# A one-token attention and MLP kernel: where the two sets of sums of the output projection meet

## The chip, the cores and the metric

The kernel runs on one core of a Trainium2 chip. The metric is the device time of one execution in microseconds (us). The profile names the engines PE (TensorE, matrix products; PEld is its weight load), DVE (VectorE), ACT (ScalarE), POOL (GpSimd) and SP (SyncE, which here only issues DMAs). A "q" behind an engine's name, as in SPq or DVEq, is that engine's instruction sequencer.

## The reference

One token `x` of 1024 numbers is normalised; an attention block and an MLP block work on the result, and both are added to `x`. Cut to what matters:

```
def reference(A_x, A_k_cache, A_v_cache, A_wq, A_wo, B_x, B_w1, B_b1, B_w2, B_b2):
    # attention: 32 query heads on 4 kv heads of 128, the last W = 4096 cache places
    #   q = xn @ wq;  p = softmax(q k^T / sqrt(128));  o = p v;  A = o @ wo
    # MLP:  y = layernorm(xn);  h = gelu(y @ w1 + b1);  B = h @ w2 + b2
    x = A_x
    xn = _layernorm(x, axis=-1)
    return x + _A_ref(xn, A_k_cache, A_v_cache, A_wq, A_wo) + _B_ref(xn, B_w1, B_b1, B_w2, B_b2)
```

`wo` is 4096 x 1024 and `w2` 3584 x 1024, both bf16. All that the output is made of ends in products of a vector with these two matrices, plus `x` and `b2`.

## The kernel before

The weights and the used parts of the caches pass through SBUF once, some 40 MB in all. SyncE issues the large loads, in this order: w1, k, wq, then (after w1 has been used) w2 and v, then (after wq has been used) wo. ScalarE issues three small loads at the start (x, b1, b2; L206 to L208). TensorE's products have the activation vector as the stationary operand, one column of it in each of 32-column strips of the array, and the matrix streams through. The functions `put`, `tile` and `full` all make their products in one line, L336: `put` uses a strip of 32 columns, so that four products in four strips can run side by side, and `full` uses all 128.

**The output projection.** wo lies in SBUF as 32 "rows", each with 128 partitions and the 1024 outputs. A row is a term of a sum with 32 terms. The rows are loaded in chunks of 16, 8, 4, 2, 1 and 1 (`WO_CHUNKS`, loaded at L193 by `load_rows`), each with a semaphore of its own, `s_wo[j]`. TensorE takes them in three ways:

- The first 24 rows run in a loop (`steps("wo", ...)`, L562), 8 at a time. SyncE releases them at L560 and L561.
- Rows 24 to 27 (chunk 2) are written out. With `row` each is two products of 512 outputs, into the accumulators `acc[0]` and `acc[1]`. These lie in two strips of partitions in PSUM bank 7 and also hold `x`, `b2` and the MLP's sums. When row 27 is done, `C["most"]` is marked.
- Rows 28 to 31 (chunks 3, 4 and 5) are four products of 256 outputs each, into `quad`, four strips of 32 partitions in the first 256 columns of PSUM bank 0. The first products into it carry the flag `start`, which resets the sums. The condition, `j == HALVES`, holds for both rows of chunk 3, 28 and 29, so that row 29 resets what row 28 has left, and row 28 isn't in the sum. The last mark is `C["fin"]`.

**The end** stands after a branch that is never taken. ScalarE copies `acc[0]` in two halves to the first two strips of 32 partitions of `PART` (an fp32 view of SBUF that lies in the tensor `KV`), and VectorE `acc[1]` to the last two (L587 and L588). Both wait for `C["most"]` only. VectorE then waits for ScalarE's copies, its own and `C["fin"]` (L589 to L591), adds `quad` and `PART` (L592) and writes `ORow` in bf16. SyncE waits for that and stores four partitions of `ORow` with 256 numbers each to the output (L594), and the program ends when the store has landed (L595).

`identf` is a 128 x 128 identity matrix in fp32, made at the start by GpSimd (L238 and L239) and used as weights or operand at L492, L501 and L534. The products at L534 (`turn_over`) write a bank that nothing reads afterwards.

Of the kernel before, what the change touches and what calls it, by code (L numbers as in the profile page):

```python
# [6 lines left out]
ALU = mybir.AluOpType  # L7
ACTF = mybir.ActivationFunctionType
# [14 lines left out]
WO_CHUNKS = [16, 8, 4, 2, 1, 1]  # L23
LOOPED = 2
HALVES = 3
# [26 lines left out]
def bass_parallel_sum__sliding_block_cached__mixer_channel_mlp__decode_kernel(  # L52
# [18 lines left out]
    pe, dve, act, pool, sp = nc.tensor, nc.vector, nc.scalar, nc.gpsimd, nc.sync  # L71

    def sems(name, n):
        return [nc.alloc_semaphore(f"{name}{i}") for i in range(n)]

    s_xrow, s_b1, s_b2, s_w1, s_w2, s_out, s_go, s_row = (
        nc.alloc_semaphore(n) for n in ("s_xrow", "s_b1", "s_b2", "s_w1", "s_w2", "s_out", "s_go", "s_row"))
# [5 lines left out]
    PE = Track(nc, "S_PE")  # L83
    DVE = Track(nc, "S_DVE")
    ACT = Track(nc, "S_ACT")
    POOL = Track(nc, "S_POOL")

    def sb(name, shape, d):
        return nc.alloc_sbuf_tensor(name, shape, d)
# [3 lines left out]
    identf = sb("identf", [128, 128], f32)  # L93
# [20 lines left out]
    ORow = sb("ORow", [128, 256], bf16)  # L114
# [21 lines left out]
    PART = KV[:, 4096:4608].bitcast(f32)  # L136
# [5 lines left out]
    PS = nc.alloc_psum_tensor("PS", [128, 8 * 512], f32)  # L142
# [9 lines left out]
    out_rows = out.rearrange("b s (a n) -> (b s a) n", a=4)  # L152

    C = {}
# [70 lines left out]
    def product(out, a, b, ready):  # L225
# [32 lines left out]
        out=SAME[:, :].rearrange("p (h b) -> p h b", b=4), in0=HD[:, 0:32].unsqueeze(2).to_broadcast([128, HQ, 4]),  # L258
        in1=HD[:, 32:64].unsqueeze(2).to_broadcast([128, HQ, 4]), op=ALU.add))
    parts = identf[:, :].rearrange("p (i q h) -> p i q h", i=NPAIR, q=4)  # L260
    POOL.mark(pool.tensor_tensor(out=HD[:, 64:128].rearrange("p (i q h) -> p i q h", i=NPAIR, q=2),
                                 in0=parts[:, :, 0:2, :], in1=parts[:, :, 2:4, :], op=ALU.add))
    pool.wait_ge(POOL.sem, POOL.cnt)
    HD4 = HD[:, 64:128].rearrange("p (i q h) -> p i q h", i=NPAIR, q=2)
    for i in range(NPAIR):
        C["consts"] = POOL.mark(pool.tensor_tensor(
            out=E4[:, :].rearrange("p (q r) -> p q r", r=129)[:, :, 64 * i:64 * i + 64:4],
            in0=HD4[:, i, 0, :].unsqueeze(1).to_broadcast([128, 4, 16]),
            in1=HD4[:, i, 1, :].unsqueeze(1).to_broadcast([128, 4, 16]), op=ALU.add))
# [65 lines left out]
    def tile(out, lhsT, rhs, size, at, load=True, start=False):  # L335
        return pe.add_instruction(mybir.InstMatmult(  # L336
            name=nc.get_next_instruction_name(), engine=pe.engine,
            ins=[lowered(rhs, False), lowered(lhsT, True)], outs=[pe.lower_ap(out)],
            start_tensor_calc=start, stop_tensor_calc=True, bass_skip_group_check=True, ldweights=load,
            tile_size=size, tile_position=at))  # L340

    def put(out, lhsT, rhs, a, load=True, start=False):
        return tile(out, lhsT, rhs, (128, 32), (0, 32 * a), load, start)

    def full(out, lhsT, rhs, load, start=False):
        return tile(out, lhsT, rhs, (128, 128), (0, 0), load, start)
# [99 lines left out]
    for eng, track, qs in ((dve, DVE, (0, 1)), (act, ACT, (2, 3))):  # L446
        eng.wait_ge(PE.sem, C["rep"])
        eng.wait_ge(POOL.sem, C["lb"])
        for q in qs:
            dst = LB8[32 * q:32 * q + 32, :, 32 * q:32 * q + 16]  # L450
            src = PS[32 * q:32 * q + 32, 6 * 512:6 * 512 + 128].rearrange("p (e h) -> p e h", e=8)
# [3 lines left out]
    def row(vec, lo, hi):  # L455
        put(acc[0], vec, lo, 0)
        return put(acc[1], vec, hi, 1)
# [10 lines left out]
    acc = [PS[32 * a:32 * a + 32, 7 * 512:8 * 512] for a in range(2)]  # L468
# [16 lines left out]
    for a in range(2):  # L485
        for i in range(2):
            src = XBR[0:1, i * D + a * 512:i * D + (a + 1) * 512]
            tile(acc[a], identb[0:1, 0:32], src, (32, 32), (0, 32 * a), i == 0, i == 0)

    for half in range(2):  # L490
# [8 lines left out]
                                       in_=MXH[:, :].unsqueeze(1).to_broadcast([1, 4, HQ]), func=ACTF.Copy))  # L499
# [5 lines left out]
    for n in range(4):  # L505
        C["exp"] = ACT.mark(act.activation(  # L506
            out=Pb[:, n * 512:(n + 1) * 512], in_=PS[:, n * 512:(n + 1) * 512], func=ACTF.Exp,
# [3 lines left out]
            out=PT.rearrange("p (i c h) -> p c i h", i=NPAIR, h=16)[:, 16 * n:16 * n + 16],  # L511
            in_=Pb[:, n * 512:(n + 1) * 512].rearrange("p (c i h) -> p c i h", i=NPAIR, h=16)))
# [27 lines left out]
    for c in range(1, 4):  # L540
        C["d_od"] = DVE.mark(dve.scalar_tensor_tensor(  # L541
            out=OD[:, :], in0=PS[:, 4 * 512 + 128 * c:4 * 512 + 128 * c + 128], scalar=BLK[:, c:c + 1], in1=OD[:, :],
# [6 lines left out]
    for dq in range(4):  # L549
# [7 lines left out]
        out=OT, in0=PS[:, 6 * 512 + 160:6 * 512 + 192], scalar1=REC[:, 0:1], scalar2=None, op0=ALU.mult))  # L557
# [7 lines left out]
    for j in range(LOOPED, len(WO_CHUNKS)):  # L565
        pe.wait_ge(s_wo[j], 16)
        for c in range(c0, c0 + WO_CHUNKS[j]):
            if j < HALVES:
                last = row(VEC[:, FC + PAD + c:FC + PAD + c + 32], WA[:, c * D:c * D + 512], WA[:, c * D + 512:(c + 1) * D])
            else:  # L570
                for a in range(4):
                    last = put(quad[a], VEC[:, FC + PAD + c:FC + PAD + c + 32], WA[:, c * D + a * 256:c * D + (a + 1) * 256], a,
                               start=(j == HALVES))
        c0 += WO_CHUNKS[j]
        if j == HALVES - 1:
            C["most"] = PE.mark(last)
    C["fin"] = PE.mark(last)

    pe.br_lt(zero, 0, on_true="L_main", on_false="L_end").branch_hint(ending)
    nc.switch_bb("L_end")  # L580

    for a in range(4):
        eng, track = ((act, ACT), (dve, DVE))[a // 2]
        eng.wait_ge(PE.sem, C["most"])
        dst = PART[32 * a:32 * a + 32, :]
        src = acc[a // 2][:, 256 * (a % 2):256 * (a % 2) + 256]
        C["part", a // 2] = track.mark(act.activation(out=dst, in_=src, func=ACTF.Copy) if eng is act  # L587
                                      else dve.tensor_copy(dst, src))  # L588
    dve.wait_ge(ACT.sem, C["part", 0])  # L589
    dve.wait_ge(DVE.sem, C["part", 1])  # L590
    dve.wait_ge(PE.sem, C["fin"])  # L591
    C["d_out"] = DVE.mark(dve.tensor_tensor(out=ORow[:, :], in0=PS[:, 0:256], in1=PART[:, :], op=ALU.add))  # L592
    sp.wait_ge(DVE.sem, C["d_out"])
    sp.dma_start(out_rows, ORow[0:128:32, :]).then_inc(s_out, 16)  # L594
    sp.wait_ge(s_out, 16)  # L595

    return nc

# [27 lines left out]
```

## Time and profile before

| what | value |
|---|---|
| median of 3 runs | 99.83 us (99.83 to 100.0) |
| profiled execution | 99.88 us |
| its span, first to last instruction | 98.6 us |
| TensorE busy | 53.6 us (54%) |
| VectorE busy | 32.8 us (33%) |
| ScalarE busy | 10.0 us (10%) |
| SyncE's DMA queue, share of 16 engines' span | 94.9% |
| read from HBM | 39.86 MB, 404 GB/s over the span |

Times in the profile count from the span's start. Busy time is summed for each engine and says nothing of order; the chain of waits goes from the last instruction back to what released it and shows what set the end. A line such as `L336` is a line of the kernel's source. In a row of the timeline the first number is the start, the second the length, and the brackets say how long the engine had been idle and what ended that. The ends of products on TensorE are modelled, not measured.

### The profile page before, as it was taken

The page shows a single profiled execution, that of the slowest core. Times are in us where ns is not written, and L with a number is a line of the kernel's source. Part 1 is how long each engine was busy: PE and PEld are TensorE (multiplying, and loading weights), DVE is VectorE, ACT ScalarE, POOL GpSimd, SP SyncE. Part 2 cuts the span into 40 slices and gives each one's busy share as a digit, 9 for nine tenths or more (in the row PEclk, how much of TensorE's full clock was granted, in tenths as well). Part 3 has the DMA queues.
Part 4 walks back from the last instruction along what each step waited for, and adds up shares of the span by engine and source line. Part 5 has one row for each costly group of instructions (what it writes and reads, how often), then busy time and mean ns, then how long its engine had stood idle before and what let it go on. Part 6 is the DMA issues. An engine that isn't in the chain of part 4 may idle for free.

```text
span 98.6 us, 970 instructions
## 1 busy us (share of the span) xinstructions
PE 53.6 (54%) x377; PEld 18.6 (19%) x297; DVE 32.8 (33%) x45; ACT 10.0 (10%) x24; POOL 10.1 (10%) x34
## 2 busy tenths in 40 slices
PE   0420300059920700760086599976999997485860
PEld 0320000012210000100010212213345544042310
DVE  0237100000799999992002300451900004100031
ACT  0506000000040000000002200005700000000030
POOL 2128996000000000000000000000000000000000
PEclk9999999999995555579556957996559999999998
DMA  9798888999999999999988899959999999999960
GB/s 373 326 422 372 373 372 372 465 425 432 425 525 439 425 425 425 425 425 425 585 372 372 372 419 674 395 213 425 425 425 425 425 425 439 425 445 402 401 227 1
DMA packets 2060, 39.86 MB, mean 404 GB/s; under 512 B 262, under 2 KB 266, under 8 KB 652
## 3 DMA queue, kind: packets, MB, share of 16 engines
q1 hardware_dynamic: 2024, 39.85, 94.9%
q10 hardware_dynamic: 36, 0.01, 0.0%
HBM read 39.86 MB, written 0.00 MB: 404 GB/s over the span
## 4 chain that ended last, share of the span: by engine, by line
DMA 88%; SPq 4%; PE 4%; issue 1%; DVE 0%; DVEq 0%
DMA WW<-in_A_wq_dram 47%; DMA WW<-in_A_wo_dram 41%; PE PS L336 4%; SPq L193 3%; SPq L201 1%; DVE ORow L592 0%; SPq L210 0%; DVEq L591 0%; SPq L372 0%
## 5 line engine op out<-in xcount | busy, mean ns | idle before, releaser
L328 DVE STREAM_TRANSPOSE KV<-KV 128x2048 bf16<-128x2048 bf16 x8 | 18.5, 2310 | 15.1 <-DMA KV<-in_A_k_cache_dram 14.9
L336 PE MATMUL PS<-WW,VEC 128*32 (+2 forms) x128 | 16.7, 421 | 4.1 <-SPq L560 1.7
L336 PE MATMUL PS<-WW,XNTb 128*32 x64 | 7.1, 623 | 12.0 <-SPq L372 12.0
L336 PE MATMUL PS<-WW,YTb 128*32 x56 | 6.3, 580 | 10.1 <-DMA WW<-in_B_w_dram 10.1
L336 PEld LDWEIGHTS PS<-WW,VEC 128*32 (+1 forms) x128 | 6.9, 107 | 14.2 <-issue 8.1
L336 PE MATMUL PS<-KV,LB 128*128 128x512 bf16 x32 | 8.8, 442 | 0.7 <-DVE LB L452 0.7
L480 DVE TENSOR_REDUCE MXP<-PS 128x1 f32<-128x1024 f32 x2 | 2.4, 1224 | 7.7 <-PE PS L336 7.7
L336 PEld LDWEIGHTS PS<-WW,XNTb 128*32 x32 | 1.2, 114 | 18.4 <-issue 18.4
L336 PEld LDWEIGHTS PS<-WW,YTb 128*32 x32 | 1.7, 121 | 14.9 <-issue 14.8
L541 DVE SCALAR_TENSOR_TENSOR OD<-PS,BLK,OD 128x128 f32<-128x128 f32 x3 | 1.1, 351 | 10.0 <-ACT OD L538 9.9
L588 DVE COPY KV<-PS 32x256 f32<-32x256 f32 x2 | 0.8, 420 | 10.3 <-PE PS L336 10.3
L336 PE MATMUL PS<-OUTM,PAR 2*128 2x512 bf16 x4 | 1.9, 615 | 3.5 <-DVE HT L399 3.5
L336 PE MATMUL PS<-KV 128*64 x32 | 3.6, 380 | 0.0
L429 DVE CAST Qs<-PS 128x512 bf16<-128x512 f32 x1 | 0.7, 691 | 8.4 <-PE PS L336 8.4
L510 DVE STREAM_TRANSPOSE KV<-KV 128x512 bf16<-128x512 bf16 x4 | 2.7, 711 | 2.0 <-ACT KV L506 2.0
L336 PEld LDWEIGHTS PS<-KV,LB 128*128 128x128 bf16 x16 | 1.8, 110 | 7.1 <-issue 6.3
L506 ACT ACTIVATE KV<-PS,BIAS 128x512 bf16<-128x512 f32 x4 | 2.7, 686 | 0.0
L336 PE MATMUL PS<-KV,oneb 1*32 1x512 bf16 x7 | 1.0, 611 | 3.0 <-DMA KV<-in_B_b_dram 3.0
L427 ACT ACTIVATE Qs<-PS 128x512 bf16<-128x512 f32 x1 | 0.6, 597 | 20.4 <-PE PS L336 20.4
L375 ACT ACTIVATE Hs<-PS 128x512 bf16<-128x512 f32 x1 | 0.6, 597 | 18.1 <-PE PS L336 18.1
L217 POOL TENSOR_SCALAR_AFFINE_SELECT OUTM<-OUTM 2x512 bf16<-2x512 bf16 x1 | 2.3, 2302 | 0.1
L534 PE MATMUL PS<-E,identf 128*128 128x512 f32 x4 | 2.2, 639 | 0.0
(93 smaller groups left out, 36.3 us busy)
## 6 DMA issues: line engine op xcount, KB each, us to landing
WW<-in_B_w_dram SPq DMA_DIRECT2D x2, 7168.0 KB, 29.4
WW<-in_A_wq_dram SPq DMA_DIRECT2D x2, 4096.0 KB, 41.8
KV<-in_A_k_cache_dram SPq DMA_DIRECT2D x2, 2048.0 KB, 26.0
KV<-in_A_v_cache_dram SPq DMA_DIRECT2D x2, 2048.0 KB, 46.0
WW<-in_A_wo_dram SPq DMA_DIRECT2D x1, 4096.0 KB, 32.5
WW<-in_A_wo_dram SPq DMA_DIRECT2D x1, 2048.0 KB, 37.1
WW<-in_A_wo_dram SPq DMA_DIRECT2D x1, 1024.0 KB, 39.1
WW<-in_A_wo_dram SPq DMA_DIRECT2D x1, 512.0 KB, 39.9
```

Of the source, the lines that this page charges most:

```text
L193: sp.dma_start(dst[:, c0 * width:(c0 + n) * width].rearrange("p (c n) -> p c n", c=n), src[:, c0:c0 + n, :],).then_inc(semaphores[j], 16)
L201: sp.dma_start(dst[:, 2 * i * W:2 * (i + 1) * W], cache[0, 2 * i:2 * i + 2, SK - W:SK, :].rearrange("g (m b) d -> m g (b d)", m=64),).then ...
L217: return POOL.mark(pool.affine_select(out=out, in_=out, pattern=pattern, compare_op=op, fill=value, base=base, channel_multiplier=step))
L328: C["kd"] = DVE.mark(dve.transpose(out=KD4[:, n], in_=KR[:, n * 2048:(n + 1) * 2048].rearrange("p (b e s) -> p b e s", b=16, e=4)))
L336: return pe.add_instruction(mybir.InstMatmult(name=nc.get_next_instruction_name(), engine=pe.engine, ins=[lowered(rhs, False), lowered(lhs ...
L429: C["d_qs"] = DVE.mark(dve.tensor_copy(Qs[:, 512:1024], PS[:, 7 * 512:8 * 512]))
L480: C["mx", half] = DVE.mark(dve.tensor_reduce(out=MXP[:, half:half + 1], in_=PS[:, half * 1024:(half + 1) * 1024], axis=AX.X, op=ALU.max))
L506: C["exp"] = ACT.mark(act.activation(out=Pb[:, n * 512:(n + 1) * 512], in_=PS[:, n * 512:(n + 1) * 512], func=ACTF.Exp, bias=BIAS[:, :], s ...
L510: C["tr", n] = DVE.mark(dve.transpose(out=PT.rearrange("p (i c h) -> p c i h", i=NPAIR, h=16)[:, 16 * n:16 * n + 16], in_=Pb[:, n * 512:(n ...
L534: pe.matmul(PS[:, 3 * 512:4 * 512], lhsT=identf[:, :], rhs=E4[:, 0:512])
L541: C["d_od"] = DVE.mark(dve.scalar_tensor_tensor(out=OD[:, :], in0=PS[:, 4 * 512 + 128 * c:4 * 512 + 128 * c + 128], scalar=BLK[:, c:c + 1] ...
L588: else dve.tensor_copy(dst, src))
```

## The change

The copies of the first sums move ahead of the last rows in the program, right behind the mark of row 27; their engines, halves and waits stay. After row 30, TensorE waits for the four copies and makes one fp32 product with the identity matrix as weights and `PART` as the streamed operand (128 x 128 by 128 x 256). It accumulates into the same 256 columns of bank 0 as `quad`, in all 128 partitions. Row 31's four products follow it. VectorE's sum is gone: ScalarE waits for `C["fin"]`, copies the 128 x 256 sums to `ORow` in bf16, waits for its own copy, issues the store from its own DMA queue and waits for it to land. VectorE and SyncE have nothing to do after the copies and the loads. The flag `start` is set for row 28 alone, so that row 28 is in the sum.

```diff
                 for a in range(4):
                     last = put(quad[a], VEC[:, FC + PAD + c:FC + PAD + c + 32], WA[:, c * D + a * 256:c * D + (a + 1) * 256], a,
-                               start=(j == HALVES))
+                               start=(c == sum(WO_CHUNKS[:HALVES])))
         c0 += WO_CHUNKS[j]
         if j == HALVES - 1:
             C["most"] = PE.mark(last)
+            for a in range(4):
+                eng, track = ((act, ACT), (dve, DVE))[a // 2]
+                eng.wait_ge(PE.sem, C["most"])
+                dst = PART[32 * a:32 * a + 32, :]
+                src = acc[a // 2][:, 256 * (a % 2):256 * (a % 2) + 256]
+                C["part", a // 2] = track.mark(act.activation(out=dst, in_=src, func=ACTF.Copy) if eng is act
+                                              else dve.tensor_copy(dst, src))
+        if j == len(WO_CHUNKS) - 2:
+            pe.wait_ge(ACT.sem, C["part", 0])
+            pe.wait_ge(DVE.sem, C["part", 1])
+            full(PS[:, 0:256], identf[:, :], PART[:, :], True)
     C["fin"] = PE.mark(last)
 
     pe.br_lt(zero, 0, on_true="L_main", on_false="L_end").branch_hint(ending)
     nc.switch_bb("L_end")
 
-    for a in range(4):
-        eng, track = ((act, ACT), (dve, DVE))[a // 2]
-        eng.wait_ge(PE.sem, C["most"])
-        dst = PART[32 * a:32 * a + 32, :]
-        src = acc[a // 2][:, 256 * (a % 2):256 * (a % 2) + 256]
-        C["part", a // 2] = track.mark(act.activation(out=dst, in_=src, func=ACTF.Copy) if eng is act
-                                      else dve.tensor_copy(dst, src))
-    dve.wait_ge(ACT.sem, C["part", 0])
-    dve.wait_ge(DVE.sem, C["part", 1])
-    dve.wait_ge(PE.sem, C["fin"])
-    C["d_out"] = DVE.mark(dve.tensor_tensor(out=ORow[:, :], in0=PS[:, 0:256], in1=PART[:, :], op=ALU.add))
-    sp.wait_ge(DVE.sem, C["d_out"])
-    sp.dma_start(out_rows, ORow[0:128:32, :]).then_inc(s_out, 16)
-    sp.wait_ge(s_out, 16)
+    act.wait_ge(PE.sem, C["fin"])
+    C["a_out"] = ACT.mark(act.activation(out=ORow[:, :], in_=PS[:, 0:256], func=ACTF.Copy))
+    act.wait_ge(ACT.sem, C["a_out"])
+    act.dma_start(out_rows, ORow[0:128:32, :]).then_inc(s_out, 16)
+    act.wait_ge(s_out, 16)
 
     return nc
```

## The prediction

> **What bounds the kernel now.** I read the chain of waits first, because only what lies on it can move the end. Its columns are start in us, length in us, and what ran.
>
> ```profile
> 55.70 40.28 DMA WW<-in_A_wo_dram
> 95.99 0.04 issue
> 96.03 0.32 PE PS L336 x4
> 96.35 0.03 issue
> 96.38 0.05 DVEq L591
> 96.43 0.04 issue
> 96.47 0.42 DVE ORow L592
> ```
>
> The kernel is bound by its loads until 95.99 us, when the last row of wo has landed. Nothing in the change issues or delays a load before that, so all that can move is the tail: the last row's four products, 0.12 us until VectorE starts (one of its waits, L591, is an instruction of its own of 0.05), the sum of 0.42, and the store. The timeline of the last 4 us shows what lies beside that tail.
>
> ```profile
> 94.90 0.37 ACT L587 ACTIVATE KV<-PS 32x256 f32<-32x256 f32 x1
> 94.95 0.42 DVE L588 COPY KV<-PS 32x256 f32<-32x256 f32 x1
> 95.40 0.10 PEld L336 LDWEIGHTS PS<-WW,VEC 128*32 128x32 bf16 x4 [0.56 <-DMA WW<-in_A_wo_dram]
> 95.40 0.29 PE L336 MATMUL PS<-WW,VEC 128*32 128x256 bf16 x4 [0.28 <-DMA WW<-in_A_wo_dram]
> 96.03 0.10 PEld L336 LDWEIGHTS PS<-WW,VEC 128*32 128x32 bf16 x4 [0.53 <-DMA WW<-in_A_wo_dram]
> 96.03 0.29 PE L336 MATMUL PS<-WW,VEC 128*32 128x256 bf16 x4 [0.34 <-DMA WW<-in_A_wo_dram]
> 96.47 0.42 DVE L592 TENSOR_TENSOR ORow<-PS,KV 128x256 bf16<-128x256 f32 x1 [1.10 <-PE PS L336]
> 96.93 0.65 SPq L594 DMA_DIRECT2D out_dram<-ORow  x1
> ```
>
> The copies end at 95.27 (ScalarE) and 95.37 (VectorE), hidden behind the loads of rows 30 and 31. Row 30's products run from 95.40 to 95.69, and TensorE is then idle until row 31 lands. That hole, 96.03 less 95.69 or 0.34 us, is what the identity product gets for nothing. The store is issued in 0.65 us, to 97.58, and SyncE's waits show the rest:
>
> ```profile
> SPq L595 <- DMA out_dram<-ORow: 1.0, 1, 1.0
> ```
>
> 97.58 and 1.02 make the span of 98.6. The profiled execution took 99.88, so 1.28 us lie outside the span; the median of the runs is 99.83, 0.05 less.
>
> **The identity product** has no row of its own size, but two fp32 products with 128x128 weights bracket it. The timeline records each as two matmuls. The first line here shows the first of such a pair, the second the pair, both with 512 columns; the third is a pair with one column.
>
> ```profile
> 81.06 0.70 PE L534 MATMUL PS<-E,identf 128*128 128x512 f32 x1
> 81.06 1.12 PE L534 MATMUL PS<-E,identf 128*128 128x512 f32 x2
> 77.18 0.38 PE L517 MATMUL PS<-SUMP,SAME 128*128 128x1 f32 x2
> ```
>
> The second of 512 columns adds 1.12 - 0.70 = 0.42, so 256 columns are 0.21 for each. The pair then is 0.70 - 0.21 + 0.21 = 0.70. A line between the pairs of 1 and 512 columns gives 0.38 + 0.74/2 = 0.75. I take 0.72.
>
> When does it start? Its waits for both copies are over at 95.37, before row 30's products begin, so they cost at most an instruction such as L591 (0.05). L534's load at 81.06 began 0.07 before the previous product ended (80.75 + 0.38 = 81.13), so I start this one 0.07 before 95.69, at 95.62, and it ends at 96.34. The bounds are 95.50, when row 30's weight loads are through, and 95.74, after its products and one wait.
>
> Row 31 is queued behind it. The timeline gives 0.29 us for four products alone and 0.40 for the eight of rows 28 and 29 back to back, so a row that streams behind another product adds 0.11. That is 96.34 + 0.11 = 96.45, or **+0.10** on the 96.35 of before. The low end is 95.50 + 0.70 + 0.11 = 96.31, which is earlier than row 31 can be done after its landing: **0**. The high end is 95.74 + 0.75 + 0.32 = 96.81, with nothing overlapped: **+0.46**. I take +0.10, since the rows with several products back to back all show overlap.
>
> **The copies** into PART are the same four instructions with the same wait, only written earlier in the program. They cost nothing more; their cover is the loads of rows 28 to 31, and without it they would cost their 0.87 us. Between VectorE's copies' end and the product's start there are 0.25 us of slack.
>
> **The wait of the last operation.** ScalarE now waits for one event, TensorE's last product, where VectorE had three waits. Two rows show ScalarE starting after a product: the copy L587 at 94.50, 0.05 after 94.45, and L538 at 81.18, 0.05 after 81.13. Against 0.12 this is **-0.07** (bounds -0.08, and 0 if a wait of 0.05 is needed here too). Nothing is queued behind that wait but the store.
>
> **The last operation.** A ScalarE copy from PSUM took 268 ns for 32x128 and 372 for 32x256, and 597 for 128x512. The increments, 104 ns for 128 columns and 225 for 256, lie on one line whatever the partitions, so 128x256 is about 0.38 instead of 0.42: **-0.04**. Bounds: 0.37, and 0.48, the middle between 367 for the 128x128 copy and 597. [...]
>
> **The store** moves from SyncE's queue to ScalarE's. SyncE's had been empty of work before it (the six wo loads were issued by 58 us), so no queue time is saved. From ScalarE's result to its own issue I take the 0.04 that VectorE to SyncE took; the only case of ScalarE waiting for itself (L503 ends at 68.11, L506 starts at 68.14) has 0.03, and one wait instruction more would add 0.05. The issue: ScalarE's three DMAs at the start took 0.52, 0.56 and 0.67, and two of them are 2 KB like the store. SyncE's 0.65 lies among these: **0**. Low bound 0.52, -0.13. High bound: both engines issued their first at 0.80 us, SyncE in 0.39 and ScalarE in 0.52; if that ratio of 1.33 were the engine's and not the shape's, the store would be 0.87, +0.22. The landing: ScalarE's x row was issued by 1.32 and first read at 2.23, so it landed within 0.91, against the store's 1.02 on SyncE; I take 1.02 unchanged, 0.1 either way. (L207's 8.3 us fell among SyncE's big loads; at the end the DMA engines are empty.)
>
> **The sum**: +0.10 - 0.07 - 0.04 + 0 = -0.01. The span becomes 98.59, its execution 99.87, and the median of runs 99.82. Adding up all the low bounds gives -0.08 - 0.05 - 0.01 - 0.13 - 0.10 = -0.37, all the high ones +0.46 + 0 + 0.06 + 0.05 + 0.22 + 0.10 = +0.89. The reset flag of row 29 costs nothing: it's a bit of products that run anyway, in the shadow of row 30's load.
>
> **The rivals.** *No overlap, slower.* The identity product takes the whole array in fp32, and row 31 starts only when it has ended. For it: L534's load started only 0.07 before the product ahead ended, and the next row after an L534 pair never follows closely in this trace. Against: after the L517 pair, which ended at 77.56, the next load and product stand at 77.49. The price is +0.46 - 0.11 = +0.35, or 100.18. It decides once the last product ends after 96.35 + 0.11 + 0.20 = 96.66.
>
> *ScalarE issues DMAs more slowly than SyncE.* The ratio of 1.33 above; +0.22 - 0.01 makes 100.04. Against it is that in the first 2 us, with both engines issuing, SyncE needed 0.60 to 0.63 and ScalarE 0.56 and 0.67.
>
> *All hidden, faster.* The identity product streams from 95.50 and is out of the way, and the store is issued in 0.52: 0 - 0.07 - 0.04 - 0.13 = -0.24, or 99.59. For it: the load of the second L534 pair began at 83.72, while L550's products ran to 83.92. [...] Against: the waits stand between row 30 and the identity product, and 0.52 was the first DMA of an empty queue.
>
> **How the numbers follow.** A measurement of this kernel can tell about 0.2%, 0.2 us, from no change. The forecast has 0.42: its own range, 99.65 to 100.0, leaves 0.34 within the bound, 0.05 below and 0.03 above. No overlap has 0.22 (0.18 slower, 0.04 within), the slow issue 0.10 (0.06 and 0.04), all hidden 0.26 (0.20 faster, 0.06 within). Together: faster 0.25, same 0.48, slower 0.27. The range reaches from a little below the faster rival, 99.50, to a little above the slower one, 100.22; the rest of the bounds, several at their ends at once, is the 2 in 10 left out.
>
> **What would show it.** In the profile after: the identity product as two fp32 matmuls of 128x256 starting near 95.6 and ending near 96.3; the last four products ending at 96.45 (96.66 or later speaks for no overlap, 96.35 for all hidden); ScalarE starting 0.05 later and taking 0.38; ScalarE's issue of 0.65; 1.0 us from there to the end. The forecast is wrong if the last wo load no longer lands near 96.0, if the copies end after the identity product could start, or if a store from ScalarE's queue lands later than one from SyncE's.

## The result and the profile after

| kernel | median | lowest to highest | runs |
|---|---|---|---|
| before | 99.89 us | 99.80 to 100.83 | 21 |
| changed | 100.21 us | 100.02 to 101.15 | 21 |

The changed kernel is slower by 0.4%: the ratio is 1.0039, with a 95% interval of 1.0021 to 1.0057. Four of its runs lie near 101.1, the others at 100.32 or below. The profiled execution is one of the four: it took 101.07, with a span of 99.7. Its chain of waits (start, length, what) ends quite differently from the one before:

```profile
86.08 0.02 SPq L560
86.09 0.55 issue
86.64 8.91 PE PS L336 x56
95.56 0.02 issue
95.58 0.42 DVE KV L583
96.00 0.03 issue
96.03 0.43 DVE KV L583
96.46 0.14 issue
96.60 0.92 PE PS L336 x6
97.52 0.02 issue
97.54 0.39 ACT ORow L594
```

From 86.6 us on no load is in the chain. TensorE runs without a pause until row 27 ends at 95.56, over 1 us later than the 94.45 of before. Then follow VectorE's two copies, the identity product and row 31 in one piece (x6: two and four products), and ScalarE's copy. The windows of this profile show why row 27 is late. Each line has the stretch, its length, then the busy time and count of TensorE, its weight loads, VectorE, ScalarE and GpSimd, and last TensorE's granted clock, the DMA engines' share and GB/s:

```profile
86.00:88.00 2.00, 1.36 (x8) 0.56 (x10) 0.00 (x0) 0.00 (x0) 0.00 (x0) 0.50 0.98 418
88.00:90.00 2.00, 2.00 (x12) 0.69 (x10) 0.00 (x0) 0.00 (x0) 0.00 (x0) 0.50 0.95 406
90.00:92.00 2.00, 2.00 (x12) 0.79 (x10) 0.00 (x0) 0.00 (x0) 0.00 (x0) 0.50 0.99 410
```

The same stretches of the profile before:

```profile
86.00:88.00 2.00, 1.43 (x14) 0.76 (x16) 0.00 (x0) 0.00 (x0) 0.00 (x0) 1.00 0.94 401
88.00:90.00 2.00, 2.00 (x22) 0.85 (x16) 0.00 (x0) 0.00 (x0) 0.00 (x0) 1.00 0.97 414
90.00:92.00 2.00, 0.74 (x8) 0.33 (x8) 0.00 (x0) 0.00 (x0) 0.00 (x0) 1.00 1.00 414
```

At a clock of 0.50 TensorE does 12 products in 2 us where it did 22, while the loads (418, 406, 410 GB/s) go on as before. So this profile has a lateness in it that begins ahead of anything the change touches. It can't show what the change costs in an ordinary run; for that the kernel was profiled again.

### The profile page after: what moved, and what is told of

Read it like the earlier page. It is cut to its first block, busy times and chain, and to the rows that moved or that the text cites. A ratio compares the mean times of both kernels' runs of the same rounds, so it can differ in the third digit from the quotient of the medians.

```text
span 99.7 us, 974 instructions
## 1 busy us (share of the span) xinstructions
PE 53.1 (53%) x379; PEld 19.1 (19%) x299; DVE 32.3 (32%) x44; ACT 10.4 (10%) x25; POOL 10.1 (10%) x34
## 4 chain that ended last, share of the span: by engine, by line
DMA 79%; PE 14%; SPq 2%; issue 1%; DVE 1%; ACT 0%
DMA WW<-in_A_wq_dram 46%; DMA WW<-in_A_wo_dram 33%; PE PS L336 14%; SPq L201 1%; DVE KV L583 1%; SPq L193 1%; ACT ORow L594 0%; SPq L210 0%; SPq L560 0%; SPq L372 0%
## 5 line engine op out<-in xcount | busy, mean ns | idle before, releaser
L336 PE MATMUL PS<-WW,VEC 128*32 (+2 forms) x128 | 15.7, 417 | 2.4 <-SPq L560 2.0
L336 PE MATMUL PS<-WW,YTb 128*32 x56 | 5.1, 493 | 10.1 <-DMA WW<-in_B_w_dram 10.1
L336 PE MATMUL PS<-KV,LB 128*128 128x512 bf16 x32 | 9.4, 466 | 0.7 <-DVE LB L452 0.7
L336 PEld LDWEIGHTS PS<-KV 128*64 x32 | 1.7, 109 | 3.0 <-issue 2.0
```

Source lines behind the costliest of these rows:

```text
L336: return pe.add_instruction(mybir.InstMatmult(name=nc.get_next_instruction_name(), engine=pe.engine, ins=[lowered(rhs, False), lowered(lhs ...
```

## The experiments

Each was run beside the kernel before on the same chip, and times are medians. Three theories were set against each other. *Product*: the identity product holds row 31 back. *Store*: ScalarE's store, or the end of the program behind it, takes longer. *Clock*: only late runs such as the one above are slower.

**The changed kernel again** (no edit).

> The changed kernel once more, for a profile in which TensorE isn't late in wo's loop (in the first profile its granted clock was 0.50 from 86 to 92 us, row 27 ended at 95.58 and the copies at 96.46). Three theories for the 0.3 us. Product: the identity product holds row 31 back by about 0.2 us in every run. Store: ScalarE's store lands later, or the program ends later behind it, by 0.1 to 0.2 us (1.13 us from the issue's end to the span's end in the first profile, against 1.02 before). Clock: only runs with the low clock in wo's loop are slower, and the others are as fast as before. All expect the profile to show the copies' end near 95.4 and row 31's landing near 96.0. Product expects the last products to end at 96.55 and a time 0.3 us above before together with the store; clock expects them to end by 96.40 and the median of the kernel within 0.1 us of before.

100.48 against 100.14; ratio 1.0047 (1.0022 to 1.0072). Three of 12 runs were at 101.27 to 101.42, the other nine at 100.28 to 100.52. This profile is of an ordinary run (100.28). Its timeline:

```profile
95.56 0.10 PEld L336 LDWEIGHTS PS<-WW,VEC 128*32 128x32 bf16 x4 [0.56 <-DMA WW<-in_A_wo_dram]
95.56 0.29 PE L336 MATMUL PS<-WW,VEC 128*32 128x256 bf16 x4 [0.28 <-DMA WW<-in_A_wo_dram]
95.79 0.30 PEld L336 LDWEIGHTS PS<-KV,identf 128*128 128x128 f32 x2
95.79 0.70 PE L336 MATMUL PS<-KV,identf 128*128 128x256 f32 x2
96.42 0.10 PEld L336 LDWEIGHTS PS<-WW,VEC 128*32 128x32 bf16 x4 [0.33 <-DMA WW<-in_A_wo_dram]
96.42 0.29 PE L336 MATMUL PS<-WW,VEC 128*32 128x256 bf16 x4
96.76 0.38 ACT L594 ACTIVATE ORow<-PS 128x256 bf16<-128x256 f32 x1 [1.32 <-PE PS L336]
97.17 0.61 ACTq L596 DMA_DIRECT2D out_dram<-ORow  x1
```

The loads land a little earlier or later in each profile (row 30 starts at 95.40 us before and at 95.56 here), so I count from row 30's load. Row 31 follows 0.86 us after it (96.42 - 95.56), where before it was 0.63 (96.03 - 95.40). The row's products then take their full 0.29 us: row 31 is **0.23** late, and it starts 0.07 before the identity product ends at 96.49. The clock theory is refuted, since the runs that aren't late are slower too.

**SyncE stores.**

```diff
-    act.wait_ge(ACT.sem, C["a_out"])
-    act.dma_start(out_rows, ORow[0:128:32, :]).then_inc(s_out, 16)
-    act.wait_ge(s_out, 16)
+    sp.wait_ge(ACT.sem, C["a_out"])
+    sp.dma_start(out_rows, ORow[0:128:32, :]).then_inc(s_out, 16)
+    sp.wait_ge(s_out, 16)
```

> The changed kernel, with the store issued and awaited by SyncE again; ScalarE still copies. Store expects the time to fall by 0.1 to 0.2 us against the changed kernel, and the stretch from the issue's end to the span's end to be 1.02 again instead of 1.13. Product expects no more than 0.05 us of difference, and the row 31 products to end as late as in the changed kernel. Clock expects no difference in the runs that aren't late.

100.37 against 100.14; ratio 1.0027 (1.0002 to 1.0051). That is 0.11 less than the changed kernel. SyncE's issue is 0.66 us instead of 0.61. To the hundredth, the traces have the span's end at 98.63 before, at 98.88 in the changed kernel and at 99.13 here. From the end of the issue to there it is 1.06 here (99.13 - 98.07) and 1.10 in the changed kernel (98.88 - 97.78); issue and landing together are 1.72 and 1.71, and 1.70 before (0.65 and 98.63 - 97.58). Inside the span, then, the store costs the same from either queue, within 0.02. What is left lies outside: each run's time less its span has a median of 1.29 us here and of 1.41 in the changed kernel. The next run shows it too.

**The kernel before, with ScalarE's store.**

```diff
-    sp.wait_ge(DVE.sem, C["d_out"])
-    sp.dma_start(out_rows, ORow[0:128:32, :]).then_inc(s_out, 16)
-    sp.wait_ge(s_out, 16)
+    act.wait_ge(DVE.sem, C["d_out"])
+    act.dma_start(out_rows, ORow[0:128:32, :]).then_inc(s_out, 16)
+    act.wait_ge(s_out, 16)
```

> The kernel before, with ScalarE issuing and awaiting the store instead of SyncE; VectorE still adds. Store expects 0.1 to 0.2 us more than before. Product and clock expect the time of before within 0.05 us.

100.28 against 100.14; ratio 1.0010 (0.9998 to 1.0022). The median span is 98.9 in both. The time outside the span has a median of 1.40 us here and of 1.26 in the 35 runs of before; for the changed kernel it is 1.41.

**ScalarE issues, SyncE waits.**

```diff
     act.dma_start(out_rows, ORow[0:128:32, :]).then_inc(s_out, 16)
-    act.wait_ge(s_out, 16)
+    sp.wait_ge(s_out, 16)
```

> The changed kernel, with ScalarE issuing the store and SyncE alone waiting for it. So far the time outside the span has been 1.26 us where SyncE issues and awaits the store, and 1.41 where ScalarE does. If it hangs on who waits last, it is 1.26 here and the kernel is 0.15 us faster than the changed one. If it hangs on who issues, it stays at 1.41 and the time doesn't change. The span itself should stay within 0.05 us of the changed kernel's by both.

100.29 against 100.21; ratio 1.0005 (0.9971 to 1.0038). The time outside the span is 1.26 again. In these kernels, then, the 0.15 us go with the engine that waits last and not with the queue; two runs below don't fit.

**No identity product.**

```diff
-            full(PS[:, 0:256], identf[:, :], PART[:, :], True)
```

> The changed kernel without the identity product; TensorE still waits for the copies. It leaves out of the output the sums of wo's first 28 rows, of the MLP, of x and of b2. Product expects the last products to end 0.2 us earlier, at 96.35, and the time to fall by 0.2 us against the changed kernel. Store expects the last products to end within 0.05 us of where they end with the product, and no change of time. Clock expects no change in the runs that aren't late.

100.23 against 100.14; ratio 1.0005 (0.9992 to 1.0017): 0.25 less than the changed kernel. Rows 30 and 31 in its timeline:

```profile
95.64 0.29 PE L336 MATMUL PS<-WW,VEC 128*32 128x256 bf16 x4 [0.28 <-DMA WW<-in_A_wo_dram]
96.32 0.13 PEld L336 LDWEIGHTS PS<-WW,VEC 128*32 128x32 bf16 x4 [0.58 <-issue]
96.35 0.29 PE L336 MATMUL PS<-WW,VEC 128*32 128x256 bf16 x4 [0.42 <-DMA WW<-in_A_wo_dram]
```

Row 31's products now start 0.71 us after row 30's. Most of the 0.23 is gone. The 0.08 that stays in this profile is put down to "issue", with two waits still standing ahead of row 31.

**A product in bf16**, with SyncE's store. PART and its copies are bf16, so the sums of the first 28 rows are rounded once more.

```diff
-    PART = KV[:, 4096:4608].bitcast(f32)
+    PART = KV[:, 4096:4352]
...
-            full(PS[:, 0:256], identf[:, :], PART[:, :], True)
+            full(PS[:, 0:256], identb[:, :], PART[:, :], True)
```

> The changed kernel with PART in bf16, so that the identity product is a single bf16 one, and with the store issued and awaited by SyncE. The copied sums are rounded to bf16 once more. Theory of the product: 128x256 in bf16 takes about 0.3 us from its weight load at 95.8 and is out of the way before row 31 lands at 96.2; the last products then end as before, and what stays of the change is ScalarE's earlier start (-0.07) and shorter copy (-0.04): 0.1 us faster than before. Rival (what delays row 31 is the waits in TensorE's queue and not the length of the product): 0.1 us slower than before.

100.09 against 100.21; ratio 0.9970 (0.9939 to 1.0000). Its timeline has row 31 at 0.61 us after row 30, where before it was 0.63:

```profile
95.83 0.29 PE L336 MATMUL PS<-WW,VEC 128*32 128x256 bf16 x4 [0.28 <-DMA WW<-in_A_wo_dram]
96.06 0.28 PE L336 MATMUL PS<-KV,identb 128*128 128x256 bf16 x1
96.44 0.29 PE L336 MATMUL PS<-WW,VEC 128*32 128x256 bf16 x4
```

The bf16 product, too, starts only 0.23 us after row 30's products, 0.06 before their end (96.06 against 96.12). So its type doesn't set its start; what bf16 saves is length, 0.28 us instead of 0.70.

The same kernel again:

> The version with the bf16 identity product and SyncE's store once more, since its interval reached 1.000. Theory: 0.1 us faster than before again, and the time outside the span 1.26. Rival: no difference, the first result having come from the runs of before near 101.

99.80 against 99.93; ratio 0.9992 (0.9976 to 1.0008). Both medians are 0.12 to 0.13 us below before. Neither interval excludes no change, so a gain isn't shown.

**A product in strips.** Why does row 31 come so long after a product of 0.70? Here four fp32 products of 32 columns of weights each do the same sum, in the strips that the rows use.

```diff
-            full(PS[:, 0:256], identf[:, :], PART[:, :], True)
+            for a in range(4):
+                put(quad[a], identf[:, 32 * a:32 * a + 32], PART[:, :], a)
```

> The changed kernel with the fp32 identity product cut into four products of 32 columns of weights, in the same strips as the rows. In all profiles so far a weight load whose product has another tile shape than the one ahead began 0.06 to 0.07 us before the end of the product ahead (95.79 against 95.85 and 96.42 against 96.49 in the changed kernel), and one of the same shape earlier (83.72 against 83.92). Theory of the shape: with the row's own shape the identity product starts within 0.15 us of row 30's products and row 31 streams behind it, so that the last products end no more than 0.1 us after where the landing would let them, and the kernel is about 0.15 us faster than the changed one. Rival (fp32 alone takes that long, whatever its shape): row 31's load still begins 0.8 us or more after row 30's, and the time is that of the changed kernel.

100.14 against 100.06; ratio 1.0003 (0.9973 to 1.0034). The changed kernel on the same chip:

> The changed kernel again, beside the one above on the same chip: 0.3 us above before, row 31's load 0.86 us after row 30's, the time outside the span 1.41, and some runs near 101.3, if the account so far holds.

100.23 against 100.06, ratio 1.0001 (0.9974 to 1.0027; four of the 23 runs of before were at 100.65 to 101.12 with 2 us or so outside their spans, which widens both intervals). Row 31 came 0.85 us after row 30 there (95.45, 96.30), the time outside the span was 1.40, and none of the 12 runs was late. The timeline with strips:

```profile
95.55 0.29 PE L336 MATMUL PS<-WW,VEC 128*32 128x256 bf16 x4 [0.27 <-DMA WW<-in_A_wo_dram]
95.65 0.19 PEld L336 LDWEIGHTS PS<-KV,identf 128*32 128x32 f32 x8
95.68 0.64 PE L336 MATMUL PS<-KV,identf 128*32 128x256 f32 x8
96.18 0.29 PE L336 MATMUL PS<-WW,VEC 128*32 128x256 bf16 x4
```

The fp32 sum now starts 0.13 us after row 30's products do, instead of 0.23, and row 31 0.14 before its end instead of 0.07. Row 31 is back at 0.63 us after row 30. Of the 0.23 us, then, 0.10 and 0.07 belong to the change between strips of 32 columns and the whole array, on the way in and on the way out, and 0.06 to the sum itself, which takes 0.64 in strips instead of 0.70.

**TensorE made late**, in both kernels: one product whose result nothing uses, ahead of row 24.

```diff
         pe.wait_ge(s_wo[j], 16)
+        if j == LOOPED:
+            turn_over()
```

> The kernel before with one more fp32 product of 128x512 (turn_over, its result unused) ahead of row 24, which makes row 27 end about 1 us later, near 95.5, as the low clock did in the first profile of the changed kernel. Theory of the late chain: before, a late row 27 delays only the copies (0.87 us), which then end near 96.4 while rows 28 to 31 run beside them, so that the sum starts at most 0.15 us later: 0 to 0.2 us above before. Rival (TensorE's lateness is passed on by both kernels alike): 0.6 to 1 us above before.

100.14 against 100.21 in the kernel before: ratio 0.9993 (0.9957 to 1.0029). Its timeline:

```profile
95.92 0.87 DVE L590 COPY KV<-PS 32x256 f32<-32x256 f32 x2 [10.10 <-PE PS L336]
96.38 0.29 PE L336 MATMUL PS<-WW,VEC 128*32 128x256 bf16 x4 [0.17 <-DMA WW<-in_A_wo_dram]
96.88 0.42 DVE L594 TENSOR_TENSOR ORow<-PS,KV 128x256 bf16<-128x256 f32 x1
```

> The changed kernel with the same product ahead of row 24. Theory of the late chain: the copies, two waits (0.1), the identity product (0.7), row 31 (0.2) and ScalarE's copy follow row 27 one after the other, so with row 27 at 95.5 the last products end near 97.4 instead of 96.7, and the time is 0.6 to 0.8 us above the changed kernel's median, 0.9 to 1.1 above before, as in the late runs near 101.3. Rival: as much later as the kernel before becomes by the same product.

101.34 in the changed kernel, from four runs only: ratio 1.0121 (1.0047 to 1.0195).

```profile
95.81 0.87 DVE L585 COPY KV<-PS 32x256 f32<-32x256 f32 x2 [10.06 <-PE PS L336]
96.83 0.67 PE L336 MATMUL PS<-KV,identf 128*128 128x256 f32 x2 [0.73 <-DVE KV L585]
97.43 0.29 PE L336 MATMUL PS<-WW,VEC 128*32 128x256 bf16 x4
97.78 0.38 ACT L596 ACTIVATE ORow<-PS 128x256 bf16<-128x256 f32 x1 [1.20 <-PE PS L336]
```

Copies that start 1.4 us late cost the kernel before nothing that its median shows: row 31 runs beside them at 96.38, and the sum starts 0.09 us after they end at 96.79. In the changed kernel row 31 stands in TensorE's queue behind the identity product, which waits for the copies and starts at 96.83; row 31 follows at 97.43. The last operation starts 1.97 us after the copies do, against 0.96.

**Is it the clock that makes the late runs?** Both kernels without the two `turn_over` products of L534:

> The kernel before without the two turn_over products, whose results nothing reads, so that TensorE is idle for longer between the attention's sums and wo's loop. Theory (the late runs near 101.3 come from a low TensorE clock in wo's loop, and only the changed kernel's chain passes the lateness on): the clock is low there in more runs, row 27 ends near 95.5 in those, and the time stays within 0.2 us of before. Rival (the clock doesn't depend on the products of L534): everything as in before, clock included.

> The changed kernel without the two turn_over products. Theory of the low clock: more than the 6 in 33 runs near 101.3 that the changed kernel has shown, with the granted clock near 0.5 in wo's loop and row 27 near 95.5 in a profile of such a run, the rest near 0.3 us above before. Rival: 2 of 12 runs near 101.3, as before.

99.92 against 99.84, ratio 0.9990 (0.9956 to 1.0024), and 100.19 against 99.84, ratio 1.0029 (0.9995 to 1.0064). The granted clock fell to 0.50 from 88 to 90 us in both profiles, but recovered in time (0.86 and 0.74 from 90 to 92), and row 27 ended before 94.8. The share of late runs didn't rise. This way of provoking them failed. That they come from a low clock rests on the one profile above and on the clocks of the single runs: in the 45 runs of the changed kernel, without an edit, seven were late, and their mean granted clock was 0.824 to 0.826 in six and 0.793 in one, while the 38 others had 0.81 or 0.827 to 0.879. The lateness goes with a clock pattern of its own; what sets the pattern is not shown.

**No second set of sums.** All rows of w2 and wo go as quarters into one set of strips; the copies, the product and VectorE's sum are gone, and SyncE stores what ScalarE copies.

```diff
     def row(vec, quarters):
         for a in range(4):
             last = put(quad[a], vec, quarters[a], a)
         return last
...
-    steps("w2", W2, 0, FC, 7)
+    steps("w2", W2, 0, FC, 4)
```

> No second set of sums at all: the rows of w2 and all rows of wo, x and b2 go as four products of 256 outputs into one set of four strips in bank 7; ScalarE waits for the last product and copies the sums, SyncE stores them. Copies, identity product and sum are gone. Theory: row 31 follows its load as before, the end is that of the bf16 version (-0.07 and -0.04), and a late row 27 delays only what stands behind it on TensorE: 0.1 us faster than before, and hardly any runs 1 us late. Rival (twice as many products and weight loads make TensorE late in wo's loop): slower than before, with row 27 ending after 94.9.

99.92 against 99.93; ratio 0.9992 (0.9974 to 1.0010). None of its 12 runs was above 100.09. TensorE's granted clock is at 0.50 at the end, where it was 1.00 in the profile before. TensorE was busy for 1.25 of the 2 us from 92 to 94, against 1.94 before; why the clock fell is not shown:

```profile
94.00:95.00 1.00, 0.75 (x16) 0.14 (x8) 0.00 (x0) 0.00 (x0) 0.00 (x0) 0.50 1.04 391
95.00:96.00 1.00, 0.70 (x16) 0.14 (x8) 0.00 (x0) 0.00 (x0) 0.00 (x0) 0.50 0.24 88
```

Row 31's products take 0.41 us instead of 0.29, about as much as ScalarE's earlier start and shorter copy save. The median span is 0.1 us shorter even so (98.6 against 98.7), but the time outside it was 1.36, against 1.24.

**Strips and SyncE's store together**, both causes taken away:

> The changed kernel with the fp32 product in four strips and the store issued and awaited by SyncE: both causes found so far taken away, fp32 kept. If they are all of the common loss, row 31's load comes 0.63 us after row 30's, the time outside the span is 1.26, and the kernel is 0.1 us faster than before, from ScalarE's earlier start and shorter copy, with a late run near 101 here and there. If something else of the change costs time in every run, it is no faster than before.

99.97 against 99.88; ratio 1.0002 (0.9978 to 1.0026). The span's median is 98.6 in both, and row 31 comes 0.62 us after row 30. But the time outside the span was 1.21 to 1.27 in five of the 12 runs, the five lowest (99.61 to 99.84), and at 1.34 or more in the others. So the time outside isn't set by the last engine alone; what else sets it stays open. No version was shown to beat the kernel before.

## Why the prediction was wrong

The median, 100.21, lay just inside the range, but the forecast was no change and the kernel became slower. That it lay inside is partly luck: half of the loss came from a term that the range didn't contain. Point by point, from row 30's load to the span's end, before against the ordinary run of the changed kernel:

| term | predicted | measured | from |
|---|---|---|---|
| row 31's products end | +0.10 | +0.23 | 96.32 - 95.40 = 0.92; 96.71 - 95.56 = 1.15 |
| from there to the last operation | -0.07 | -0.10 | 0.15; 96.76 - 96.71 = 0.05 |
| last operation | -0.04 | -0.04 | 0.42; 0.38 |
| to the issue | 0 | -0.01 | 0.04; 0.03 |
| issue | 0 | -0.04 | 0.65; 0.61 |
| landing | 0 | +0.05 | 98.63 - 97.58 = 1.05; 98.88 - 97.78 = 1.10 |
| span | -0.01 | +0.09 | 3.23; 3.32 |
| outside the span | 0 | +0.15 | medians of 1.26 and 1.41 |

The span's ends are those of the traces; the prediction's landing of 1.02 came from an end rounded to 98.6. It also counted row 31's end before as 96.35, the chain's, where the timeline has 96.32: that moves 0.03 between the first two lines, so that of the first line's miss 0.10 are real, and the second was forecast right.

0.09 + 0.15 = 0.24 us, from one profile of each kernel. Between the medians lie 0.32 and 0.34. Without the late runs, four in 21 and three in 12, the changed kernel's medians are 100.16 and 100.45, 0.27 and 0.31 above before. What is left of these, 0.03 and 0.07, stays unexplained.

- **Right**: the identity product's own size (0.72 predicted, 0.70 measured) and its start 0.07 us before row 30's end (measured 0.06); ScalarE's start 0.05 after the last product, its copy of 0.38, the bounds of issue and landing; and since issue and landing together came to 1.70 and 1.71, the store itself as unchanged. The rival of a slow issue by ScalarE fell: 0.61 against 0.65.
- **Wrong, the step "a row that streams behind another product adds 0.11"**: it took 0.22, since row 31's load began 0.07 us before the product's end and the row then took its 0.29. The 0.11 came from rows 28 and 29, two products of the same tile shape. The profile before had the right row, and it was quoted in the prediction as evidence of overlap: after the pair of L517 the next load, of another shape, stood at 77.49, 0.07 before the pair's end. The bf16 product and the strips showed that the shape was most of it: of the 0.23 us, 0.17 went with the strips. In six transitions to another shape, listed in the last section, the load began only 0.06 to 0.07 us before the end of the product ahead. The load at 83.72 that the prediction cited for "all hidden", 0.20 before the end of L550's products at 83.92, had the shape of the products ahead (128 x 128), and the identity product, behind row 30's strips, did not. The rival "no overlap" had the mechanism nearly right, but with +0.35 it was too dear, because each load did start 0.07 before the end ahead of it. Row 31's products ended 1.15 us after row 30's load, halfway between the forecast's 1.05 and the 1.26 (96.66 - 95.40) that was to speak for the rival.
- **Wrong, "1.28 us lie outside the span"**, taken as a constant. The move of the last wait from SyncE to ScalarE made it 0.15 us longer, half of the loss. The prediction had priced the store's issue and landing but not the program's end. What takes the 0.15 us is not shown.
- **Missing: the slack of 0.25 us ahead of the identity product.** It was told as a margin, without asking what follows when row 27 is later than that. Seven of 45 runs of the changed kernel had spans of 99.5 us or more (the expectations above count one too few); of the 149 runs of before beside the experiments none was above 99.2. The late pair shows why: the chain behind row 27 had become 1 us longer (1.97 against 0.96 from the copies' start to the last operation's), and only the loads' pace hid it. So the step that the copies' cover costs nothing failed in some of the runs: their wait became part of the chain.

## What to carry to other kernels

Work put into a hole of one engine's queue must be priced with its entry and its exit, from rows of the same tile shapes: here the change of shape cost 0.10 us on the way in and 0.07 on the way out. Ahead of the last load it must not wait for what can be late: here the chain behind row 27 was hidden in the ordinary profile, and with row 27 made late it took 1.97 us from the copies' start to the last operation's, against 0.96 before. And the engine that ends the program is part of the change: the runs' time less the span, 1.26 us before and 1.41 in the changed kernel, is a term of the sum.

## What the runs showed that I had not expected

- In six transitions between tile shapes the next weight load began 0.06 to 0.07 us before the modelled end of the product ahead: 77.49 against 77.56, 81.06 against 81.13, 64.82 against 64.89 and 65.36 against 65.42 before, 95.79 against 95.85 and 96.42 against 96.49 in the changed kernel. With one shape throughout, a load began 0.20 before (83.72 against 83.92), and fp32 strips 0.19 before (95.65 against 95.84).
- In all eight measurements, of six kernels, in which ScalarE waited last the median time outside the span was 1.40 to 1.44 us. Where SyncE did, it was 1.24 to 1.29, but for the quarters (1.36) and the strips with SyncE's store (1.37), whose runs spread from 1.20 upwards.
- The store took 1.70 to 1.72 us from the start of its issue to the span's end in all 17 profiles: SyncE's issue was 0.05 longer than ScalarE's (0.65 or 0.66 against 0.61) and its landing 0.05 shorter (1.05 or 1.06 against 1.10 or 1.11).
- The granted clock was 0.50 for 6 us of wo's loop (86 to 92) in the changed kernel's first profile, and row 27 ended at 95.56. In its second profile it was 0.57 from 86 to 90 us and 1.00 from 90 to 94, and the copies behind row 27 started in time, at 94.67.
